# Attention with routing hidden in it: the logits' sum, the squares and the mixing moved within their units

## The chip, the cores and the metric

One core of a Trainium2 chip runs the whole program. The metric is the device time of the core in microseconds (us). The median of three runs of the kernel before is 892.65 us (891.91 to 894.43).

## What is computed

The reference is attention with a memory term, followed by two layers of experts:

```python
scores = scale * q @ k.T                      # 4 batches, 8 heads, 576 rows, depth 64; causal mask
a = softmax(scores); local = a @ v
mem_out = (phi(q) @ M_prev) / (phi(q) @ z_prev + 1e-6)   # phi(x) = max(x, 0) + exp(min(x, 0))
x = g * mem_out + (1 - g) * local             # 2304 rows of 512
# first layer: logits = (x / |x|) @ (emb / |emb|).T / tau, 8 experts; the best expert per row
# second layer: logits = x @ w_gate; both: gate * (relu(x @ w1[e]) @ w2[e])
```

## The kernel before

The attention stage works on 16 pairs of heads (four batches of four pairs). A pair has ten units: its rows are cut in four chunks of 128 and one of 64 leftover rows, and each chunk is taken for the two heads in turn, in the order 4, 0, 3, 2, 1, where chunk 4 is the leftover one. The unit numbers run on over all pairs, ten to a pair. All instructions of the stage are issued in an order written out by hand: for each step `s` the letters of one string are gone through, and each letter issues the work of one phase for the unit that has reached it.

- `s`: the scores of unit `s` on TensorE (`pss`), and the masked minimum on VectorE (`mins`, L209; it subtracts, masks and reduces in one instruction).
- `x`: the exponential of unit `s-1` on ScalarE (L244).
- `n`: the reciprocal of the row sums of a pair, two steps after its last unit.
- `a`: unit `s-3`: transposes of the exponentials on TensorE (`psat`, L261) and their copy on ScalarE (`att`, L263).
- `v`: unit `s-4`: the value product on TensorE (`psav`, L284). At the pair's third unit the leftover rows' value product (`pslo`, L281: ten float32 products, each two instructions) stands in front; its fifth and tenth product read that unit's own copy `att`, the others an earlier one.
- `c`: five steps behind: the mixing. For the leftover rows (`emit_combl`) four small VectorE steps on `pslo` and an addition; for the whole pair (`emit_comb`) a multiplication of the value product by the reciprocals on VectorE (`tmp`, L295) and the addition of the memory term on GpSimd (`xb`, L296). After a batch's last pair SyncE stores the mixed rows (L344).
- `e` and `p`: events on the other engines and on TensorE, filed under a step: loads, transposes of q and k on VectorE (L138), phi on GpSimd and ScalarE (L142, L146, L148), the memory product (`psm`, L165) and its division on VectorE (`memx`, L184), and the routing of the batch before.

Each engine takes its instructions in the order in which they were issued. The events share two PSUM slots (tag `t`) in turn: a new user waits until the last user of its slot has been read. `pslo` takes one of these slots too, in phase `v`.

The routing of the first layer for a batch is filed in `Hooks.events` for the first three batches, counted from `base`, the step in which the batch's last pair is mixed: squares of the rows on ScalarE (L1024), a square root on GpSimd (`norm1`), six VectorE steps (`norm2`), the logits as parts and their sum (`parts_pe`, `sum_pe`) with a copy (L962), five steps of `choose`, the ranks (`rank_pe`, `rank_ev`), the count (L652, L653), and seven steps of `gates`, whose first ends in a tanh on ScalarE (L626). The third batch (`last`) goes on to pick the most wanted expert (`pick_pe`, `pick`, `pick_last`), to place its rows (`place_`), to load its weights and to gather its rows. `steps(s, g, n, per)` files a generator's steps, `per` of them in each unit. The fourth batch has squares of its own, filed one unit after its third pair's mixing, at the end of `events`.

After attention come the two layers of experts, one group of 128 rows after another, bound by TensorE.

Of the kernel before, what the change touches and what calls it, by code (L numbers as in the profile page):

```python
# [20 lines left out]
def tile_attention(tc, q, k, v, M_prev, z_prev, beta, ident, x1, xp, hooks):  # L21

    nc = tc.nc
# [352 lines left out]

    W = dict(a=do_at, c=do_comb, s=do_s, x=do_exp, n=do_norm, e=do_ew, p=do_pe, v=do_av)
    for s in range(-24, U + LC + 1):
        for f in "ceaspnvx":
            W[f](s)  # L380
    ctx.close()
    pctx.close()
# [3 lines left out]
def tile_kernel(ctx, tc, q, k, v, M_prev, z_prev, beta, emb, tau, w1a, w2a, wg, w1b, w2b, out):  # L386
    nc = tc.nc
    B, H, S, D = q.shape
    E, DM, FF = w1a.shape
# [106 lines left out]
    def rtile(shape, nm, dt=F32):  # L496
        return rt.tile(shape, dt, tag=nm, name=nm)
# [60 lines left out]
    def place_(c0, n):  # L558

        sl = slice(c0, c0 + n)  # L560
        ri = rtile([P, 8], "ri", I32)[:, 0:n]
        r2 = rtile([P, 8], "r2", I32)[:, 0:n]
        rk = rtile([P, 8], "rk")[:, 0:n]
        V = nc.vector
        V.tensor_copy(ri, rkb[:, sl])
        yield
        V.tensor_scalar(out=r2, in0=ri, scalar1=7, scalar2=None, op0=ALU.arith_shift_right)
        yield
        V.tensor_scalar(out=ri, in0=ri, scalar1=127, scalar2=None, op0=ALU.bitwise_and)
        yield  # L570
        V.tensor_copy(tq[:, sl], r2)
        yield
        V.tensor_copy(rk, ri)
        yield
        V.tensor_tensor(out=ohp[:, sl], in0=iop.unsqueeze(1).to_broadcast([P, n, P]), in1=rk.unsqueeze(2).to_broadcast([P, n, P]), op=ALU.is_equal)
# [82 lines left out]
    is0, not0, isl, oth = (rtile([P, E], x) for x in ("is0", "not0", "isl", "oth"))  # L658
# [5 lines left out]
    def pick(L, cnt):  # L664

        V = nc.vector
        m0, k8 = rtile([P, 2], "m0"), rtile([P, E], "k8")
        V.tensor_reduce(out=m0[:, 0:1], in_=cnt, axis=AX.X, op=ALU.max)
        yield
        V.scalar_tensor_tensor(out=k8, in0=cnt, scalar=m0[:, 0:1], in1=ioer, op0=ALU.is_equal, op1=ALU.mult)  # L670
        V.tensor_scalar(out=nl3, in0=thr, scalar1=m0[:, 0:1], scalar2=0.0, op0=ALU.is_ge, op1=ALU.add, accum_out=nul)
        yield

        V.scalar_tensor_tensor(out=q3, in0=nl3, scalar=-99.0, in1=iot[:, 0:NE], op0=ALU.mult, op1=ALU.add)
        V.tensor_reduce(out=m0[:, 1:2], in_=k8, axis=AX.X, op=ALU.max)
        yield
        V.tensor_scalar(out=is0, in0=k8, scalar1=m0[:, 1:2], scalar2=None, op0=ALU.is_equal)
        V.tensor_scalar(out=not0, in0=k8, scalar1=m0[:, 1:2], scalar2=None, op0=ALU.not_equal)
        V.tensor_scalar(out=ini[:, L, 0:1], in0=m0[:, 1:2], scalar1=-1.0, scalar2=float(E), op0=ALU.mult, op1=ALU.add)

    def pick_last(cnt):
        V = nc.vector
        m0, k8 = rtile([P, 2], "m0"), rtile([P, E], "k8")
        V.tensor_tensor(out=k8, in0=cnt, in1=not0, op=ALU.mult)
        yield
        V.tensor_reduce(out=m0[:, 0:1], in_=k8, axis=AX.X, op=ALU.max)
        yield
        V.scalar_tensor_tensor(out=k8, in0=k8, scalar=m0[:, 0:1], in1=ioer, op0=ALU.is_equal, op1=ALU.mult)
        yield
        V.tensor_reduce(out=m0[:, 1:2], in_=k8, axis=AX.X, op=ALU.max)  # L690
        yield
        V.scalar_tensor_tensor(out=isl, in0=k8, scalar=m0[:, 1:2], in1=not0, op0=ALU.is_equal, op1=ALU.mult)
        yield
        V.tensor_tensor(out=oth, in0=not0, in1=isl, op=ALU.subtract)
# [223 lines left out]
    class Hooks:  # L918
        def events(self, pe, ew, o, ps_t, at, xb_t, xl_t):

            self.ps = {}
            self.xT = {}
            self.xb_t, self.xl_t = xb_t, xl_t
            slot = lambda nm: ps_t.tile([P, 512], F32, tag="t", name=nm)
            g = setup_gates(ps_t, xp)
            ew(1, g[0])
            ew(12, g[1])
            ew(18, g[2])
            pe(25, g[3])
            ew(26, g[4])  # L930
            for i, f in enumerate(consts()):
                ew(20 + i, f)
            for pi in range(4 * B - 1):
                b, n = divmod(pi, 4)
                sc = 10 * pi + o
                pe(sc + 6, lambda b=b, n=n: self.x_pe(b, n, slot("psxt")))
                ew(sc + 6 + 1, lambda b=b, n=n: self.x_ev(b, n, 1))
                if b % 2 == 1 and n > 0:
                    ns = range(n - 1 if n == 1 else n, n + 1)
                    d = 5 if n < KD - 1 else 4  # L940
                    pe(sc + d, lambda b=b, ns=ns: self.xl_pe(b, ns, slot("psxl")))
                    ew(sc + d + 1, lambda b=b, ns=ns: self.xl_ev(b, ns, 1))
            for b in range(B - 1):
                base = 10 * (4 * b + 3) + o
                r = Route1(*self.cols(b))
                r.rows = self.rows(b)
                for i in range(r.n):
                    ew(base + (1 + i if i < 4 else 4), lambda b=b, i=i: self.square(b, i))
                ew(base + 6, r.norm1)
                pe(base + 8, lambda b=b: self.parts_pe(b, slot("pslp")))  # L950
                ew(base + 9, lambda b=b: self.parts_ev(b))
                pe(base + 11, lambda b=b: self.sum_pe(b, slot("pslg")))

                last = b == B - 2

                def steps(s, g, n, per=1):
                    for i in range(-(-n // per)):
                        m = min(per, n - per * i)
                        ew(s + i, lambda m=m: [next(g, None) for _ in range(m)])

                lg = r.d8
                ew(base + 12, lambda b=b, lg=lg: nc.vector.tensor_copy(lg, self.lg(b)))  # L962
                steps(base + 13, r.choose(lg), 5)
                steps(base + 7, r.norm2(), 6)
                pe(base + 18, lambda r=r: r.rank_pe(slot("psr")))
                ew(base + 19, r.count)
                steps(base + 19, r.rank_ev(), 2)
                steps(base + (16 if last else 21), r.gates(), 7)
                if last:
                    steps(base + 21, place_(r.i0, r.n), 6, 2)  # L970
                    pe(base + 19, lambda: self.pick_pe(slot("pspk")))
                    cnt = oth
                    ew(base + 20, lambda: nc.vector.tensor_copy(cnt, self.ps["pk"][:, 0:E]))
                    steps(base + 21, pick(0, cnt), 4)
                    ew(base + 25, self.first_expert)
                    for c in range(8):
                        ew(base + 25 + c, lambda c=c: self.first_load(c))
                    steps(base + 25, pick_last(cnt), 6)
                    g = self.g = early(0, r.i0 + r.n, self.idx_ps)
                    steps(base + 25, g, 5)  # L980
                    pe(base + 30, lambda: self.idx_pe(slot("psid")))
                    ew(base + 31, lambda: drain(self.g))
                    ew(base + 32, lambda: gather(0, 0))
                else:
                    steps(base + 28, place_(r.i0, r.n), 6)

            b = B - 1
            pe(10 * (4 * b + 1) + o + 9, lambda: self.part_pe(slot("pslp")))
            ew(10 * (4 * b + 1) + o + 9 + 1, self.part_ev)
            for i in range(5):  # L990
                ew(10 * (4 * b + 2) + o + 1 + i, lambda i=i: self.square(b, i, slice(0, P * (KD - 1))))
# [146 lines left out]
    def rows_of(t):  # L1138

        return xgt[t % 2] if t else xg0  # L1140

    def gather(L, t):
        rows = src[L] if t >= NE else src[L][0:1 + P * (NT1 - (5, 2)[L])]
        return nc.gpsimd.indirect_dma_start(out=rows_of(t), out_offset=None, in_=rows, in_offset=bass.IndirectOffsetOnAxis(ap=idx[:, L, t:t + 1], axis=0))  # L1144

    def drain(g):
        for _ in g:
            pass

    xca = [ctile([P, 4], f"xca{i}") for i in range(2)]  # L1150
    xcb = ctile([P, 4], "xcb")
    hooks = Hooks()
    tile_attention(tc, q, k, v, M_prev, z_prev, beta, ident, x1[:, 0:DM], xp, hooks)


# [30 lines left out]
    steps = {}  # L1186
# [355 lines left out]
    b = Bufs(lambda i: Wh[0][:, 1, 512 * i:512 * i + 512] if i < 6 else None)  # L1542
# [89 lines left out]
    s, b, c = steps[1, 0], bufs, NS - 1  # L1632
# [107 lines left out]
```

## Time and profile before

| | |
|---|---|
| median of the runs | 892.65 us |
| the profiled execution | 894.2 us, its span 892.4 us |
| TensorE busy (share of the span) | 858.1 us (96%) |
| VectorE busy | 507.8 us (57%) |
| ScalarE busy | 474.4 us (53%) |
| GpSimd busy | 276.4 us (31%) |
| mean granted TensorE clock | 0.990 of full speed |

PE is TensorE (PEld its weight loads), DVE VectorE, ACT ScalarE, POOL GpSimd, SP SyncE. An idle time in brackets is that of the engine just before the instruction, with the instruction that ended it; L1024 is line 1024. Matmuls are pipelined, and the ends in their rows are modelled.

### The profile page before, as it was taken

Reading aid. Unit: us, or ns where it says so; the run is one execution under the profiler, and the core shown is the slowest. Engines: PE = TensorE matmul, PEld = TensorE weight load, DVE = VectorE, ACT = ScalarE, POOL = GpSimd, SP = SyncE. Lnnn points to the kernel's source line nnn. Section 1 sums busy time; section 2 is a strip of 40 time slices with the busy share of each in tenths; the row PEclk is TensorE's granted clock in tenths of the full one; section 3 lists DMA queues with packets and bytes.
Section 4 is the critical chain, followed back from the end, with each engine's and each line's share of the span. In section 5 each row is a group of like instructions: output and inputs, shape, how many; then the busy total and the mean of one; then the engine's idle time right before and its main releaser. Section 6 shows DMA issues by size and latency. Waiting matters only on the chain. (4 is left out here: it accounts for less than half of the span.)

```text
span 892.4 us, 20618 instructions
## 1 busy us (share of the span) xinstructions
PE 858.1 (96%) x5187; PEld 675.0 (76%) x5187; DVE 507.8 (57%) x1589; ACT 474.4 (53%) x940; POOL 276.4 (31%) x375
## 2 busy tenths in 40 slices
PE   5999999999999999999999999999989999999996
PEld 2777677777668777877888877877868888888885
DVE  5657567568575866387536676644466414463520
ACT  3657657667566635376545545432366425564531
POOL 5457636536531111221221221211132112321221
PEclk9999999999999999999999999999999999999998
DMA  8424453423215266188424317022688415384111
GB/s 131 82 44 95 79 169 94 83 45 84 55 23 204 71 225 214 49 270 274 145 79 127 106 47 228 27 51 56 220 264 276 139 48 156 128 303 131 44 38 40
DMA packets 139813, 110.30 MB, mean 124 GB/s; under 512 B 107258, under 2 KB 107258, under 8 KB 139652
## 3 DMA queue, kind: packets, MB, share of 16 engines
q1 hardware_dynamic: 129252, 85.03, 33.3%
q0 software_dynamic: 8032, 23.22, 7.9%
q8 instruction: 53, 0.87, 0.4%
q14 instruction: 108, 0.88, 0.3%
q10 hardware_dynamic: 2368, 0.30, 0.2%
HBM read 90.32 MB, written 19.25 MB: 123 GB/s over the span
## 5 line engine op out<-in xcount | busy, mean ns | idle before, releaser
L1235 PE MATMUL py<-Wh,b 128*128 (+1 forms) x688 | 240.7, 406 | 2.5 <-DVE b L1179 2.4
L1235 PE MATMUL ph<-Wh,b 128*128 (+1 forms) x672 | 227.9, 400 | 0.7 <-ACTq L1246 0.7
L901 DVE TENSOR_TENSOR Wl<-stg,Wh 128x1024 f32 (+1 forms) x120 | 145.4, 1224 | 81.7 <-ACT Wh L898 71.7
L1235 PEld LDWEIGHTS py<-Wh,b 128*128 128x128 f32 x688 | 129.3, 188 | 32.5 <-issue 4.7
L1235 PEld LDWEIGHTS ph<-Wh,b 128*128 128x128 f32 x672 | 126.8, 189 | 27.1 <-ACTq L1246 1.1
L898 ACT ACTIVATE Wh<-stg 128x1024 f32 (+1 forms) x120 | 125.6, 1058 | 25.9 <-DVEq L1246 7.5
L1235 PE MATMUL py<-Wl,b 128*128 (+1 forms) x344 | 134.8, 392 | 0.0
L1235 PE MATMUL ph<-Wl,b 128*128 (+1 forms) x336 | 131.9, 392 | 2.1 <-DVEq L1246 2.0
L1179 DVE TENSOR_TENSOR b<-pt,b 128x512 fp32r<-128x512 f32 x86 | 59.4, 691 | 104.1 <-ACT b L1178 103.2
L263 ACT ACTIVATE att<-psat 128x512 f32<-128x512 f32 (+1 forms) x144 | 66.6, 463 | 78.2 <-PE psat L261 77.4
L284 PE MATMUL psav<-vb,att 128*128 128x128 f32 (+1 forms) x640 | 97.6, 283 | 0.9 <-ACT att L263 0.8
L284 PEld LDWEIGHTS psav<-vb,att 128*128 128x128 f32 x640 | 81.7, 192 | 20.9 <-ACT att L263 9.9
L1342 POOL DMA_INDIRECT out_dram<-ysb,xca x21 | 26.9, 1282 | 192.4 <-ACTq L1246 122.9
L1178 ACT ACTIVATE b<-pt 128x512 fp32r<-128x512 f32 x86 | 51.5, 598 | 62.9 <-PE pt L1347 61.7
L244 ACT ACTIVATE a<-a,mx 128x128 f32<-128x128 f32 (+3 forms) x128 | 71.0, 555 | 9.6 <-DVE mx L209 9.6
L1235 PEld LDWEIGHTS ph<-Wl,b 128*128 128x128 f32 x336 | 63.7, 190 | 14.8 <-DVEq L1246 2.7
L1235 PEld LDWEIGHTS py<-Wl,b 128*128 128x128 f32 x344 | 64.9, 189 | 9.8
L1337 ACT ACTIVATE ysb<-py,xca 128x512 f32<-128x512 f32 x42 | 28.8, 686 | 76.1 <-PE py L1235 65.4
L1144 POOL DMA_INDIRECT xg<-x_scratch,idx x48 | 55.9, 1165 | 40.5 <-POOL xca L1331 11.2
L209 DVE CUSTOM_DVE_ANT_0 a<-pss,wmask 128x128 f32<-128x128 f32 (+3 forms) x128 | 60.6, 478 | 9.0 <-PE pss L231 6.7
L1459 POOL DMA_DIRECT2D x_scratch<-xcb x21 | 11.9, 566 | 163.4 <-DVEq L1246 61.6
L261 PE MATMUL psat<-ident,a 128*128 128x128 f32 x320 | 58.2, 280 | 0.7 <-ACT a L244 0.6
(376 smaller groups left out, 1246.5 us busy)
## 6 DMA issues: line engine op xcount, KB each, us to landing
stg<-in_moe_w_dram SPq DMA_DIRECT2D x120, 512.0 KB, 4.9
x_scratch<-ysb POOLq DMA_DIRECT2D x22, 256.0 KB, 2.8
qkn<-in_q_dram SPq DMA_DIRECT2D x64, 72.0 KB, 2.5
qkn<-in_k_dram SPq DMA_DIRECT2D x60, 72.0 KB, 2.4
vb<-in_v_dram SPq DMA_DIRECT2D x32, 128.0 KB, 2.3
x_scratch<-xb SPq DMA_DIRECT2D x16, 256.0 KB, 3.3
x_scratch<-stg SPq DMA_DIRECT2D x11, 258.0 KB, 3.8
xg<-x_scratch,idx POOLq DMA_INDIRECT x48, 4.1
```

The lines of the kernel that those rows point to most:

```text
L209: nc.vector.tensor_tensor_reduce(out=out, in0=ps, in1=mask, scale=-0.125, scalar=bound, op0=ALU.add, op1=ALU.min, accum_out=m)
L244: nc.scalar.activation(out=a[:, 0:N], in_=a[:, 0:N], func=AF.Exp, scale=-1.0, bias=mx, accum_out=rs_t[pi][:, c, j:j + 1])
L261: nc.tensor.transpose(ps[:, 128 * i:128 * i + 128], x, ident)
L263: nc.scalar.activation(out=att[:, 0:N], in_=ps[:, 0:N], func=AF.Copy)
L284: nc.tensor.matmul(av_t[pi][:, c, j:], att[:, 128 * kb:128 * kb + 128], vn[:, kb, j:, 0:D], start=(kb == 0), stop=(kb == c))
L898: return nc.scalar.activation(out=chunk(Wh, c, wv), in_=stg[:, c].unsqueeze(1), func=AF.Copy).ins
L901: return nc.vector.tensor_tensor(out=chunk(Wl, c, wv), in0=stg[:, c].unsqueeze(1), in1=chunk(Wh, c, wv).bitcast(F32), op=ALU.subtract).ins
L1144: return nc.gpsimd.indirect_dma_start(out=rows_of(t), out_offset=None, in_=rows, in_offset=bass.IndirectOffsetOnAxis(ap=idx[:, L, t:t + 1] ...
L1178: nc.scalar.activation(out=hi, in_=ps, func=AF.Copy)
L1179: nc.vector.tensor_tensor(out=lo, in0=ps, in1=hi.bitcast(F32), op=ALU.subtract)
L1235: mm = nc.tensor.matmul(ps, x[:, col:col + P], W, start=(first and q_ == qs[0]), stop=(last and q_ == qs[-1]))
L1337: nc.scalar.activation(out=ysb, in_=py, func=AF.Copy, scale=xc[:, 0:1])
```

## The change

Three things are moved; no arithmetic changes. Step numbers count from `base`.

- The order of the phases in a step is `eascpnvx` instead of `ceaspnvx`: the mixing `c` is issued behind the unit's scores and masked minimum, the events `e` come first.
- The squares stand at 1, 3, 5, 7 and 9 instead of 1, 2, 3, 4 and 4; the square root at 11 instead of 6, `norm2` from 12 instead of 7.
- The sum of the logits stands at 13 instead of 11, its copy at 14, `choose` from 15 instead of 13; in the third batch it takes two steps a unit. The ranks stand at 20 (17 in the third batch) instead of 18, `rank_ev` and the count one unit later, `gates` from 21 (18 in the third batch, two steps a unit, instead of 16). In the third batch the pick stands at 18 instead of 19, and all behind it one unit sooner.

```diff
-        for f in "ceaspnvx":
+        for f in "eascpnvx":
...
-                    ew(base + (1 + i if i < 4 else 4), lambda b=b, i=i: self.square(b, i))
-                ew(base + 6, r.norm1)
+                    ew(base + 1 + 2 * i, lambda b=b, i=i: self.square(b, i))
+                ew(base + 11, r.norm1)
...
-                pe(base + 11, lambda b=b: self.sum_pe(b, slot("pslg")))
+                pe(base + 13, lambda b=b: self.sum_pe(b, slot("pslg")))
...
+                steps(base + 12, r.norm2(), 6)
                 lg = r.d8
-                ew(base + 12, lambda b=b, lg=lg: nc.vector.tensor_copy(lg, self.lg(b)))
-                steps(base + 13, r.choose(lg), 5)
-                steps(base + 7, r.norm2(), 6)
-                pe(base + 18, lambda r=r: r.rank_pe(slot("psr")))
-                ew(base + 19, r.count)
-                steps(base + 19, r.rank_ev(), 2)
-                steps(base + (16 if last else 21), r.gates(), 7)
+                ew(base + 14, lambda b=b, lg=lg: nc.vector.tensor_copy(lg, self.lg(b)))
+                steps(base + 15, r.choose(lg), 5, 2 if last else 1)
+                k = base + (17 if last else 20)
+                pe(k, lambda r=r: r.rank_pe(slot("psr")))
+                steps(k + 1, r.rank_ev(), 2, 2 if last else 1)
+                ew(k + 1, r.count)
+                steps(base + (18 if last else 21), r.gates(), 7, 2 if last else 1)
                 if last:
-                    steps(base + 21, place_(r.i0, r.n), 6, 2)
-                    pe(base + 19, lambda: self.pick_pe(slot("pspk")))
+                    pe(base + 18, lambda: self.pick_pe(slot("pspk")))
...
-                    steps(base + 21, pick(0, cnt), 4)
+                    steps(base + 20, pick(0, oth), 4)
+                    steps(base + 20, place_(r.i0, r.n), 6, 2)
...
```

## Rows read from the trace of the kernel before

**Rows 1.** Stages view, the attention stage: stretch, its length, busy time (instructions), clock, DMA

```profile
24.00:288.00 264.00, 258.84 (x2034) 192.42 (x2032) 174.23 (x702) 172.04 (x483) 137.14 (x169) 0.99 0.38 88
```

**Rows 2.** Waits of TensorE, 24 to 290 us: us in total, times, longest

```profile
PE pslo L281 <- PE pss L231: 1.5, 2, 1.0
PE pslo L281 <- issue: 1.4, 1, 1.4
PE psav L284 <- ACT att L263: 0.8, 1, 0.8
PE psat L261 <- ACT a L244: 0.6, 2, 0.4
PE pss L231 <- DVE mx L209: 0.3, 1, 0.3
PE psm L165 <- DVE memx L184: 0.3, 1, 0.3
```

**Rows 3.** Stages view, 235 to 245 us; the clock is third from the end

```profile
235.00:240.00 5.00, 3.59 (x29) 2.88 (x28) 4.51 (x15) 2.63 (x7) 5.00 (x5) 0.89 0.05 11
240.00:245.00 5.00, 5.00 (x39) 4.38 (x39) 2.51 (x10) 2.12 (x6) 2.24 (x4) 0.77 0.01 3
```

**Rows 4.** Timeline of all engines, 82 to 86 us: first batch's last mixing and first square

```profile
82.18 0.69 DVE L295 TENSOR_TENSOR tmp<-psav,rs 128x512 f32<-128x512 f32 x1 [1.27 <-PE psav L284]
82.51 1.13 PE L231 MATMUL pss<-kT,qT 64*128 64x512 f32 x4
...
82.96 1.28 POOL L296 TENSOR_TENSOR xb<-tmp,memx 128x512 f32<-128x512 f32 x1 [5.11 <-DVE rn L176]
...
83.57 0.33 PE L261 MATMUL psat<-ident,a 128*128 128x128 f32 x1
...
84.20 1.67 POOL L142 TENSOR_SCALAR ph<-qT 128x576 f32<-128x576 f32 x1
84.20 0.69 DVE L209 CUSTOM_DVE_ANT_0 a<-pss,wmask 128x512 f32<-128x512 f32 x1
84.27 0.63 ACT L1024 ACTIVATE mv<-xb 128x512 bf16<-128x512 f32 x1 [0.61 <-POOL xb L296]
...
84.81 0.77 DVE L138 STREAM_TRANSPOSE kT<-qkn 128x576 f32<-128x576 f32 x1
84.90 0.36 ACT L263 ACTIVATE att<-psat 128x256 f32<-128x256 f32 x1
...
85.79 0.62 PE L281 MATMUL pslo<-vb,att 128*64 128x65 f32 x7
```

**Rows 5.** Timeline of TensorE, first and third batch's pslo: start, us, instruction, idle before

```profile
104.65 1.35 PE L281 MATMUL pslo<-vb,att 128*64 128x65 f32 x20 [0.96 <-PE pss L231]
107.40 0.49 PE L231 MATMUL pss<-kT,qT 64*128 64x256 f32 x2
...
239.11 2.40 PE L281 MATMUL pslo<-vb,att 128*64 128x65 f32 x20 [1.41 <-issue]
...
243.33 0.49 PE L231 MATMUL pss<-kT,qT 64*128 64x256 f32 x2
```

**Rows 6.** Timeline, 187 to 189 us: second batch's first step of the gates

```profile
187.60 0.16 DVE L625 TENSOR_TENSOR d<-d,sc 128x40 f32<-128x40 f32 x1
...
187.94 0.37 ACT L263 ACTIVATE att<-psat 128x256 f32<-128x256 f32 x1
188.18 0.62 PE L281 MATMUL pslo<-vb,att 128*64 128x65 f32 x7
```

**Rows 7.** Timeline, 250 to 259 us: third batch's ranks and count, then a placing step

```profile
250.23 0.78 DVE L138 STREAM_TRANSPOSE qT<-qkn 128x576 f32<-128x576 f32 x1
...
250.75 0.19 PE L617 MATMUL psr<-oh,tri 128*128 128x32 bf16 x1
...
251.32 0.20 DVE L652 TENSOR_REDUCE ca<-oh 128x8 f32<-128x32 bf16 x1
...
251.63 0.17 DVE L653 TENSOR_TENSOR acc<-acc,ca 128x8 bf16<-128x8 bf16 x1
251.71 0.18 DVE L645 TENSOR_TENSOR t<-oh,psr 128x32 f32<-128x32 bf16 x1
...
258.77 0.98 DVE L569 TENSOR_SCALAR ri<-ri 128x4 int32<-128x4 int32 x1
```

More of the change, by code (lines that the diff above doesn't have):

```diff
@@ L968, in events @@
-                steps(base + (16 if last else 21), r.gates(), 7)
-                if last:
-                    steps(base + 21, place_(r.i0, r.n), 6, 2)
-                    pe(base + 19, lambda: self.pick_pe(slot("pspk")))
-                    cnt = oth
-                    ew(base + 20, lambda: nc.vector.tensor_copy(cnt, self.ps["pk"][:, 0:E]))
-                    steps(base + 21, pick(0, cnt), 4)
-                    ew(base + 25, self.first_expert)
+                ew(base + 14, lambda b=b, lg=lg: nc.vector.tensor_copy(lg, self.lg(b)))
@@ new lines, in events @@
+                steps(base + 15, r.choose(lg), 5, 2 if last else 1)
[4 more added lines that the diff above has]
+                steps(base + (18 if last else 21), r.gates(), 7, 2 if last else 1)
+                if last:
+                    pe(base + 18, lambda: self.pick_pe(slot("pspk")))
+                    ew(base + 19, lambda: nc.vector.tensor_copy(oth, self.ps["pk"][:, 0:E]))
+                    steps(base + 20, pick(0, oth), 4)
+                    steps(base + 20, place_(r.i0, r.n), 6, 2)
+                    ew(base + 24, self.first_expert)
@@ L976, in events @@
                     for c in range(8):
-                        ew(base + 25 + c, lambda c=c: self.first_load(c))
-                    steps(base + 25, pick_last(cnt), 6)
+                        ew(base + 24 + c, lambda c=c: self.first_load(c))
+                    steps(base + 24, pick_last(oth), 6)
                     g = self.g = early(0, r.i0 + r.n, self.idx_ps)
-                    steps(base + 25, g, 5)
-                    pe(base + 30, lambda: self.idx_pe(slot("psid")))
-                    ew(base + 31, lambda: drain(self.g))
@@ L983, in events @@
-                    ew(base + 32, lambda: gather(0, 0))
+                    steps(base + 24, g, 5)
+                    pe(base + 29, lambda: self.idx_pe(slot("psid")))
+                    ew(base + 30, lambda: drain(self.g))
+                    ew(base + 31, lambda: gather(0, 0))
                 else:
```

## The prediction

> **What bounds the kernel now.** I first read the page's shares: TensorE is busy 96% of the span, no other engine over 57%. Then the attention stage alone [rows 1]: 258.84 of 264 us, and all that the diff moves is issued there, so only TensorE's gaps in that stage count. The view of waits names them [rows 2]: three waits of the leftover rows' value product (pslo), 2.9 us together, one of a value product for a copied attention tile (0.8), and three small ones of 0.3 to 0.4 in the third batch's routing. One pslo wait (0.5) stands at a place that the diff leaves alone. The chain of waits I left aside: it ends in the last stage, at work that merely runs earlier or later with the end of attention. Last the clock [rows 3]: 1.00, then 0.89 and 0.77 in the two stretches behind the longest gap, a piece of some 3.4 us at the lower level (0.11 and 0.23 of 5 us, doubled).
>
> What a gap is worth: TensorE works in order, so a gap that goes moves the end by itself, unless another comes behind it. An idle time in these rows counts from the modelled end of the matmul before. The next could have started sooner, as in [rows 4], where the product at 82.51 ends by its row at 83.64 and its successor runs on time at 83.57. By starts the gaps are 0.1 to 0.4 longer; for the six gaps below I add 1.0 us in all (estimate).
>
> **Logits' sum two units later.** pslo, sum and the memory product share two PSUM slots in turn. With the sum in front, pslo takes the slot of the second memory product, which VectorE has yet to read; behind it, pslo takes the first one's, read two units before. Away go 0.96 us in the first batch and 1.41 in the third [rows 5]; the second shows none, since five tiles' logits stand there as cover. What is late next is the sum: its slot is read in the unit before it, so I cost it at nothing (if that read ran late, at most the old 0.96). The sum's matmuls are the same ones. Behind the 1.41 gap came the slow stretch: from pslo to the next scores 4.22 us, against 2.75 in the first batch, whose gap of 0.96 left the clock full [rows 5]. I let the drop go: 1.47 us more. Bounds: 0 if another drop replaces it, 1.47.
> The Trainium skill (TensorE: Matmul & The Clock Gate, HAM oscillation) takes half of the throttled time as the loss. By that rule the 3.4 us would give 1.7 instead of the rows' 1.47, and the sum would be 0.2 us better.
>
> **Squares in every other unit.** In the second batch they stood four units in a row and two in one unit, and the 0.8 us wait for ScalarE's copy came there [rows 2]. Apart, this goes: 0.77. Three like it, under the view's threshold, I leave to the range (0.1 to 0.3 each). The square root, normalization and choice come up to six units later; nothing on TensorE waits for them before the ranks.
>
> **Mixing behind the minimum.** This is the costly part. In the unit that is `base`, VectorE mixed at 82.18, GpSimd added till 84.24, and the first square, at the head of ScalarE's next unit, waited for that add [rows 4]. Behind it in ScalarE's queue stands the attention copy at 84.90, done at 85.26. The leftover product reads it with its ninth matmul of twenty (20 take 1.35 [rows 5], so 0.5 after the first): needed at 86.3, a spare 1.0 us.
> Now the mixing stands behind the minimum. The scores end at 83.64, the minimum starts at 83.70 and hands on after 0.61 (84.20 to 84.81): mixing at 84.31, 2.13 later. Add 0.78 later and 1.28 long, to 86.37; the copy starts 0.66 after that (84.24 to 84.90), takes 0.36, ends 87.39. TensorE waits from 86.3: 1.1 us. GpSimd's own `min` (1.67), which now precedes the add, fits in the 5.11 us idle. There are three such places, one a batch; the same steps from the mixings at 149.44 and 216.12 give 1.3 and 1.1: 3.5 in sum. The fourth batch's squares, which the diff leaves as they are, also begin one unit after a mixing (273.02); that stretch ran at the lower clock, so between 0 and 1.3, taken 0.7. Bounds for all four: 0 to 5. Elsewhere a later mixing is read six units on: nothing. Minima start up to 1 us sooner, which no wait of TensorE asks for outside the third batch. SyncE's four stores of the mixed rows start 2.1 us later and the value loads behind them too, ten units ahead of use: nothing.
>
> **Gates, ranks, count.** The gates' tanh heads ScalarE's unit, again ahead of the copy that pslo reads. In the second batch VectorE gave it at 187.60, the copy ended at 188.31 and was needed at 188.7: 0.35 spare [rows 6]. In front of it now come the mixing (0.69; the minimum, bound by its scores, can't move up) and the rank's product and the count's two steps (251.32 to 251.71 and 0.1: 0.5) [rows 7]. 1.2 less 0.35 is 0.85. In the first batch the minimum can move up 0.7, and the same sum leaves 0.4. So 1.3; bounds 0 to 2.
> Third batch: the pick's matmul comes in the unit of the count. TensorE is there some 0.15 us after 250.75; VectorE transposes from 250.23 for 0.7, then rank and count end near 251.65 [rows 7]: 0.8 us of wait, bounds 0.4 to 1. In exchange the three waits of 0.3, 0.3 and 0.4 [rows 2] are redrawn: the one-hot rows and small steps (some 1.5 us) now precede the minimum for which the scores wait, some 0.9 us of other steps come earlier. I let the three go (1.0) and put one wait of 1.0 in their place, bounds 0.5 to 1.9. First weight loads and the gather start a unit sooner on SyncE's and GpSimd's queues; nothing reads them before attention ends, so I cost them at nothing.
> VectorE's small steps have a second price too: 0.98 us for four elements a partition at 258.77, where eight at 251.63 take 0.17 [rows 7]. GpSimd was multiplying at that time. The normalization now runs in the units in which GpSimd works without pause.
> The Trainium skill (SBUF — State Buffer, Who interferes with whom) has VectorE and GpSimd share a port pair under an exclusive lock. [...]
> I put this at nothing, since VectorE's minima there have about 1.5 us before their copies are asked for (estimate), and keep 3 us as a bound.
>
> **Sum.** Gained: gaps 0.96 + 1.41 + 0.77 + 1.0 = 4.14, by starts 1.0 more, clock 1.47: 6.6. Lost: 3.5 + 0.7 + 1.3 + 0.8 + 1.0 = 7.3. Net 0.7 slower. The profiled execution took 894.2 us (span 892.4 and 1.8 around it), so 894.9 there. It is 1.55 above the median of the runs, about the price of one stretch at the lower clock; on the median of 892.65 the forecast is **893.3 us**, no change that can be told: 0.3%, about 2.7 us, is what a measurement of this kernel can tell from none.
>
> **Rivals.**
> 1. *The squares' wait is hidden, faster.* If TensorE has other work there, or the add comes sooner, 3.5 + 0.7 are not paid: 893.3 - 4.2 = 889.1. For it: ScalarE waited 0.61 us for this add before and TensorE none. Against: only 1.0 us was spare, and the shift is twice that. Chance 0.15.
> 2. *The new gaps drop the clock, slower.* Five new gaps of about 1 us stand where work was dense. A gap of 1.41 was followed by the lower clock, one of 0.96 was not; the new ones lie between, and two more drops would cost 2.9: 896.2. It decides at the first pslo behind a square. Chance 0.12.
> 3. *VectorE locked out beside GpSimd, slower.* Six normalization steps in each of three batches; if one in three takes 0.8 us more (0.98 less 0.17) in front of a minimum and half reaches TensorE: 6 x 0.8 / 2 = 2.4, to 895.7. Chance 0.08. The rule named above would bring this about.
> 4. *The change doesn't do what it says.* pslo still waits in the first and third batch, for the copy or another slot, and the drop stays: 0.96 + 1.41 + 1.47 come back, 897.1. Chance 0.08.
> The forecast has 0.57; by its own bounds it lies from 891 to 895.5.
>
> **How the numbers follow.** The range runs from 889.2, which all but reaches rival 1, to 896.8, over rivals 2 and 3. Faster: 0.14 of rival 1 and 0.02 of the forecast, 0.16. Slower: rivals 2 and 4, half of 3, and 0.01 of the forecast, 0.25. Within 0.3%: the rest, 0.59.
>
> **What would show it.** Right: no idle time before pslo at the unit of the old 104.65 and 239.11; the square's row with an idle time of about 2.7 us released by GpSimd's add, and behind it pslo split with a gap of about 1 us, three times; the pick's matmul waiting for VectorE's acc; clock 1.00 around 235 to 245. Wrong: pslo unbroken behind the squares (rival 1), or more stretches at the lower clock than before (rival 2).

## The result, and the profile after

| | before | new kernel |
|---|---|---|
| median of the runs | 892.43 us (891.91 to 894.43, 4 runs) | 901.2 us (899.8 to 901.37, 4 runs) |
| ratio to before, 95% interval | | 1.0091 [1.0072, 1.0109] |
| profiled execution, its span | 894.2, 892.4 us | 901.37, 899.6 us |
| TensorE busy | 858.1 us | 859.0 us |
| first attention score to the next stage's first matmul | 279.4 us | 286.5 us |

The forecast was 893.3 us, its range ended at 896.8. TensorE does the same work; 7.0 of the 7.2 us by which the spans differ were lost in the attention stage. In its stages view (stretch, length, busy time and instructions of TensorE, its weight loads, VectorE, ScalarE, GpSimd; clock, DMA share, GB/s) the stretch is 7 us longer than in [rows 1], TensorE busy for as long as there:

```profile
24.00:295.00 271.00, 259.29 (x2030) 192.06 (x2029) 176.01 (x699) 170.69 (x482) 139.29 (x169) 0.99 0.37 86
```

The new kernel's waits of TensorE, the same view as [rows 2] (us in total, times, longest):

```profile
PE pslo L281 <- ACT att L263: 4.6, 5, 1.2
PE psat L261 <- ACT a L244: 1.8, 6, 0.8
PE pslp L1050 <- DVE memx L184: 1.2, 1, 1.2
PE pss L231 <- DVE mx L209: 1.2, 1, 1.2
PE pslo L281 <- issue: 1.1, 1, 1.1
PE pspk L662 <- DVE acc L653: 1.0, 1, 1.0
PE psm L165 <- POOL mz L157: 0.6, 1, 0.6
```

The old list added up to 4.9 us, this one to 11.5. None of the old large waits is in it: pslo's waits for its slot in the first and third batch and the 0.8 for a copied tile are gone. But the leftover product now waits five times for ScalarE's copy.

In the timeline of TensorE the first and the third batch's pslo run without idle time and at full speed (1.38 us in place of the 2.40 in [rows 5]), with the sum behind them:

```profile
104.85 1.38 PE L281 MATMUL pslo<-vb,att 128*64 128x65 f32 x20
...
106.92 0.96 PE L1068 MATMUL pslg<-sel,xT 128*128 128x8 f32 x8
...
241.55 1.38 PE L281 MATMUL pslo<-vb,att 128*64 128x65 f32 x20
...
243.62 0.96 PE L1068 MATMUL pslg<-sel,xT 128*128 128x8 f32 x8
```

The all-engine timeline of the place of [rows 4], the unit behind the first batch's last pair:

```profile
83.49 1.13 PE L231 MATMUL pss<-kT,qT 64*128 64x512 f32 x4
...
84.65 0.69 DVE L209 CUSTOM_DVE_ANT_0 a<-pss,wmask 128x512 f32<-128x512 f32 x1 [0.69 <-PE pss L231]
...
85.27 0.69 DVE L295 TENSOR_TENSOR tmp<-psav,rs 128x512 f32<-128x512 f32 x1
...
86.04 1.27 POOL L296 TENSOR_TENSOR xb<-tmp,memx 128x512 f32<-128x512 f32 x1 [2.62 <-DVE tmp L295]
...
86.55 0.68 PE L281 MATMUL pslo<-vb,att 128*64 128x65 f32 x8
...
87.34 0.63 ACT L1024 ACTIVATE mv<-xb 128x512 bf16<-128x512 f32 x1 [2.71 <-POOL rkb L448]
...
87.97 0.36 ACT L263 ACTIVATE att<-psat 128x256 f32<-128x256 f32 x1
...
88.39 0.91 PE L281 MATMUL pslo<-vb,att 128*64 128x65 f32 x12 [1.16 <-ACT att L263]
```

Read it from the bottom: the last twelve matmuls wait for the copy, the copy stands behind the square, the square behind GpSimd's add (it ends at 87.31), the add behind the mixing, the mixing behind the minimum, the minimum behind the scores. (The square's row names a memset of rkb, which stands directly behind the add. In E3 below the square runs 1.65 us ahead of that memset, so it is the add that counts.) The mixing starts 1.78 us behind the start of the unit's scores, where in [rows 4] it stood 0.33 ahead of it. Of these 2.1 us about 0.6 are the minimum itself, and the other 1.5 its wait for the scores. The same gap stands at 156.00 (1.17) and 225.08 (1.16).

Where it went, pair by pair: the time from one pair's first score matmul to the next pair's (us; the last to the next stage's first matmul), worked out from the traces of five kernels, E2, E5 and E10 being experiments below. E10's trace is of its slowest run (890.64 us at a mean clock of 0.990), while six of its eight runs lie between 885.8 and 887.3 us at 0.993 or more, so its column holds more of the lower clock than its median does. Pairs with less than 0.1 us of difference between before and new are left out.

| pair | what stands there | before | new | E2 | E5 | E10 |
|---|---|---|---|---|---|---|
| 2 | unit 26, slot of the second memory product | 16.57 | 17.17 | 17.16 | 16.57 | 16.56 |
| 4 | first square, batch 1 | 16.22 | 17.31 | 17.31 | 16.05 | 16.04 |
| 5 | pslo and sum, batch 1 | 18.35 | 17.41 | 17.41 | 17.40 | 17.40 |
| 6, 7 | ranks and tanh, batch 1 | 32.69 | 32.89 | 32.89 | 32.02 | 32.02 |
| 8 | first square, batch 2 | 16.96 | 17.38 | 17.37 | 15.59 | 15.58 |
| 9 | fifth square, sum, batch 2 | 18.25 | 19.13 | 19.14 | 19.14 | 18.30 |
| 10 | ranks and tanh, batch 2 | 15.79 | 16.95 | 16.95 | 16.08 | 16.07 |
| 12 | first square, batch 3 | 16.20 | 17.31 | 17.31 | 16.05 | 16.05 |
| 13 | pslo and sum, batch 3 | 20.36 | 17.41 | 17.40 | 17.41 | 17.41 |
| 14 | pick, placing, batch 3 | 18.11 | 19.89 | 21.54 | 19.30 | 18.97 |
| 15 | index product, batch 4's squares | 22.83 | 26.55 | 22.81 | 23.55 | 24.47 |

Pairs 5 and 13 give back 3.9 us, as forecast; all others lose 10.9. In pairs 14 and 15 the clock moves as well: 3.4 us at half in pair 15 before, 6.8 in pair 15 of the new kernel and of E10, 3.4 in pair 14 of E2 and in pair 15 of E5. In the new kernel's stages view it is these two rows (clock third from the end; 0.27 and 0.41 of 5 us, doubled, are 6.8 us):

```profile
275.00:280.00 5.00, 4.59 (x30) 4.29 (x32) 0.78 (x4) 0.02 (x1) 0.00 (x0) 0.73 0.93 348
280.00:285.00 5.00, 5.00 (x19) 2.62 (x20) 2.85 (x9) 1.35 (x4) 1.51 (x2) 0.59 0.03 11
```

So the attention stage holds as much of the lower clock as before: 3.4 us in pair 13 and 3.4 in pair 15 there, 6.8 in pair 15 here.

Three of the places had no term in the sum. The fifth square, moved to `base + 9`, reads the second batch's leftover rows xl (one buffer); GpSimd's add into xl waits for it, behind the add stands a multiply for the memory product:

```profile
166.85 0.62 ACT L1024 ACTIVATE mv<-xl 128x512 bf16<-128x512 f32 x1
...
167.63 0.45 POOL L296 TENSOR_TENSOR xl<-tmp,memx 64x128 f32<-64x128 f32 x1 [7.96 <-ACT mv L1024]
...
168.05 0.39 POOL L157 TENSOR_TENSOR mz<-mz,gt 128x128 f32<-128x128 f32 x1
...
168.49 0.86 PE L165 MATMUL psm<-mz,ph 128*128 128x130 f32 x4 [0.57 <-POOL mz L157]
```

The index product, a unit sooner, shares its unit with the memory product and the fourth batch's partial logits (L1050): three users of two PSUM slots, so the third waits for VectorE to read the first's (memx, 274.64 for 0.62). TensorE's rows:

```profile
273.08 0.75 PE L165 MATMUL psm<-mz,ph 128*128 128x130 f32 x4
273.76 0.48 PE L714 MATMUL psid<-mvh,ohp 128*128 128x6 bf16 x13
275.41 2.68 PE L1050 MATMUL pslp<-enT,xT 128*128 128x8 f32 x20 [1.16 <-DVE memx L184]
```

And unit 26, where the wait of 0.52 us that I had left out of account, the diff being elsewhere, became 1.12: VectorE now mixes ahead of the reading of that slot.

```profile
54.87 0.56 DVE L184 TENSOR_TENSOR memx<-psm,rn 128x384 f32<-128x384 f32 x1
...
55.53 1.35 PE L281 MATMUL pslo<-vb,att 128*64 128x65 f32 x20 [1.12 <-issue]
```

### The profile page after: what moved, and what is told of

Read it like the earlier page. It is cut to its first block, busy times and chain, and to the rows that moved or that the text cites. A ratio compares the mean times of both kernels' runs of the same rounds, so it can differ in the third digit from the quotient of the medians.

```text
span 899.6 us, 20635 instructions
## 1 busy us (share of the span) xinstructions
PE 859.0 (95%) x5187; PEld 675.2 (75%) x5187; DVE 509.8 (57%) x1589; ACT 473.2 (53%) x940; POOL 277.4 (31%) x375
```

## The experiments

Theory A: the later mixing is the cost, and the rest of the change is a gain. Rivals: the routing's new units are the cost (B); single steps of it are (slot, fifth square, pick). The kernel before was timed again on the chips of the experiments (medians 893.9 to 894.1 us), so ratios are what to compare. Diffs are against the new kernel unless it is said otherwise.

**E1, the order alone, in the kernel before.**

```diff
-        for f in "ceaspnvx":
+        for f in "eascpnvx":
```

> The kernel before with nothing but the order of the phases of the change (events first, mixing behind the minimum). Theory A (the later mixing is the main cost: the first square of a batch waits for it on ScalarE, and pslo for ScalarE, 1.2 to 1.4 us in each of three batches, and VectorE reads the memory products later): 897 to 899 us, with pslo split by a gap of about 1.1 us behind the first square of each batch. Theory B (the main cost is the third batch's routing, packed two steps a unit and with one more user of the two PSUM slots in unit 153): within 1 us of the kernel before, 892 to 893.5.

Measured: 904.32 us, ratio 1.0127 [1.0101, 1.0153]. A, and more than its 897 to 899 us: by the medians the order alone costs more than the whole change, though the intervals touch. Its waits of TensorE:

```profile
PE pslo L281 <- ACT att L263: 4.9, 5, 1.2
PE pslo L281 <- issue: 4.1, 3, 1.5
...
```

The waits for the slot that the later sum removes (0.96 and 1.41 before) are 1.47 each here. The lower clock comes four times in attention, against twice before: behind both of these waits (107.5 and 250.9 us), and at 179.2 and 285.0.

**E2, the index product, its drain and the gather a unit later (as before).**

```diff
-                    pe(base + 29, lambda: self.idx_pe(slot("psid")))
-                    ew(base + 30, lambda: drain(self.g))
-                    ew(base + 31, lambda: gather(0, 0))
+                    pe(base + 30, lambda: self.idx_pe(slot("psid")))
+                    ew(base + 31, lambda: drain(self.g))
+                    ew(base + 32, lambda: gather(0, 0))
```

> The changed kernel with the index product, its reading and the gather back where they were (one unit later), nothing else. Theory B: in the changed kernel unit 153 has three users for two PSUM slots, and the fourth batch's partial logits wait 1.16 us for VectorE there, and the clock then falls for 6.8 us. So the gap before L1050 goes and the lower clock with it or half of it: 897.5 to 899 against 901.2. Theory A: the gap goes, the clock falls all the same (it did before, in 3.4 us): 899.5 to 900.

Measured: 898.06 us, ratio 1.0060 [1.0036, 1.0084], against 1.0091: about 3 us, though the intervals overlap and within its theory B's 897.5 to 899 (B is the slot here). By the traces it is 2.1 us in pairs 1 to 15, and 1.5 of it is the lower clock. The wait of 1.16 us in front of L1050 is gone and pair 15 has no stretch at the lower clock; one of 3.4 us stands in pair 14 instead. With this wait gone the fourth batch's square shows its own gap, 0.72 us in pslo at 282.53.

**E3, E2 with the old order of the unit.**

```diff
-        for f in "eascpnvx":
+        for f in "ceaspnvx":
```

> As e2, and with the old order of the phases too (mixing first). Against e2: Theory A: 5 us faster or more, 893 to 894.5, no gap within pslo behind the squares, no wait before the pslo of unit 26 beyond the 0.5 us of before. Theory B: within 1.5 us of e2.

Measured: 889.53 us, ratio 0.9964 [0.9945, 0.9983]: faster than the kernel before, and 8.5 us below E2. That is theory A, though its 893 to 894.5 us was some 4 us too high. No pslo is split behind a square or a tanh beyond 0.2 us, unit 26 waits 0.52 us as before. What is left, by its waits of TensorE:

```profile
PE pss L231 <- DVE mx L209: 1.5, 2, 1.1
PE pspk L662 <- DVE acc L653: 0.7, 1, 0.7
PE psid L714 <- DVE memx L184: 0.6, 1, 0.6
...
```

**E4, the fifth square at its old unit.**

```diff
-                    ew(base + 1 + 2 * i, lambda b=b, i=i: self.square(b, i))
+                    ew(base + (1 + 2 * i if i < 4 else 4), lambda b=b, i=i: self.square(b, i))
```

> The changed kernel with the square of the leftover rows back at base + 4. Theory: the leftover rows of all batches share one buffer, so that GpSimd's addition for the next batch waits for this square, and GpSimd's scaling of the memory term behind it came late: a gap of 0.57 us before psm in the second batch. It goes: 0.6 us faster than the change, 900.6. Rival: the gap has another cause (the normalization) and stays: 901.2.

Measured: 900.27 us, ratio 1.0082 [1.0056, 1.0108]. Against the new kernel's 1.0091 this can't be told by time; by the trace the wait of psm is gone and pair 9 takes 18.30 us in place of 19.13, while pair 8, where the square now stands, takes 0.27 more.

**E5, E2 with the mixing between the attention copies and the minimum.**

```diff
-        for f in "eascpnvx":
+        for f in "eacspnvx":
```

> E2 (the new kernel, index product, its copy and its gather a unit later: 898.1 us, ratio 1.006) with the mixing put between the attention's copy and the unit's masked minimum, so that it still stands behind the routing's steps but no longer behind the minimum; E3 has it ahead of all three (889.5 us, ratio .9964). Theory A1: it is the masked minimum alone, some 1.2 us of VectorE ahead of the mixing and of everything read behind it, that costs the 8.5 us: the time comes to 889 to 891 us and the half-clock stretches and the gaps within the leftover product go as in E3. Rival A2: the routing's steps ahead of the mixing cost as much, since a square or a small step then also delays it: 893 to 896 us. Rival A3: any place behind the routing's steps costs it all: 897 to 899 us.

Measured: 889.12 us, ratio 0.9954 [0.9937, 0.9971]: A1. That the mixing stands behind the routing's steps costs nothing that can be told from E3; that it stands behind the minimum costs all. One stretch at the lower clock is left (3.4 us in pair 15), against A1's words. Its waits of TensorE have no copy behind a square any more:

```profile
PE pspk L662 <- DVE acc L653: 1.0, 1, 1.0
PE pss L231 <- DVE mx L209: 0.9, 1, 0.9
PE psat L261 <- ACT a L244: 0.8, 4, 0.2
...
```

The minimum itself takes 0.69 us. The larger part of the price is its wait for the scores (1.5 us at the place shown above): everything queued behind it on VectorE waits too.

**E6, the first four squares one unit later.**

```diff
-                    ew(base + 1 + 2 * i, lambda b=b, i=i: self.square(b, i))
+                    ew(base + (2 + 2 * i if i < 4 else 9), lambda b=b, i=i: self.square(b, i))
```

> The new kernel with the first four squares of a batch one unit later each (units 2, 4, 6, 8 behind the base in place of 1, 3, 5, 7; the fifth stays at 9). Theory A: the three gaps of 1.16 us within the leftover product come from the first square alone, which now stands in the unit of the mixing and ahead of the attention's copy; with it out of that unit they and the .2 us gaps behind them go, 3 x (1.16 + .2) = 4.1 us, and the time comes to 896.5 to 898 us against 901.2. Rival: the copy of the next unit waits for the square as long, the gap only moves, 900 to 902 us. Also under theory A: the tanh split, the unit-26 wait of 1.12 us and the third batch's tail stay as they are.

Measured: 896.05 us, ratio 1.0040 [1.0016, 1.0065]: theory A, just below its 896.5. Pairs 4, 8 and 12 take 15.77, 15.84 and 15.77 us: 1.54 less each, 4.6 in all. In the timeline pslo is whole, and the square, which now comes behind the copy that pslo reads, has kept ScalarE idle for 0.58 us where it was 2.71:

```profile
84.28 1.28 POOL L296 TENSOR_TENSOR xb<-tmp,memx 128x512 f32<-128x512 f32 x1 [2.62 <-DVE tmp L295]
...
84.79 1.38 PE L281 MATMUL pslo<-vb,att 128*64 128x65 f32 x20
...
85.60 0.63 ACT L1024 ACTIVATE mv<-xb 128x512 bf16<-128x512 f32 x1 [0.58 <-POOL rkb L448]
```

**E7, E2 with the pick and all behind it a unit later too (as before).**

```diff
-                    pe(base + 18, lambda: self.pick_pe(slot("pspk")))
-                    ew(base + 19, lambda: nc.vector.tensor_copy(oth, self.ps["pk"][:, 0:E]))
-                    steps(base + 20, pick(0, oth), 4)
-                    steps(base + 20, place_(r.i0, r.n), 6, 2)
+                    pe(base + 19, lambda: self.pick_pe(slot("pspk")))
+                    ew(base + 20, lambda: nc.vector.tensor_copy(oth, self.ps["pk"][:, 0:E]))
+                    steps(base + 21, pick(0, oth), 4)
+                    steps(base + 21, place_(r.i0, r.n), 6, 2)
...
```

> The new kernel with the pick of the third batch, what stands behind it and the index product each one unit later, as in the kernel before (order of the unit unchanged). Includes E2's edit, which alone gave 898.1 us. Theory A: the pick's wait of .97 us at 253.8 goes or falls to .3, the third batch's two late waits (.76 and 1.15 us) fall by at least half, and the time comes to 896 to 897.3 us. Rival: these waits come from the mixing behind the minimum and from the choice two units apart, not from the pick's place: no change against E2, 897.7 to 898.5 us.

Measured: 895.93 us, ratio 1.0024 [1.0011, 1.0037]. Theory A, at its lower end. The pick's wait is gone: the 0.26 us that E9's text below puts down to it stands in front of the value product behind the pick, which waits for an attention copy. The scores' wait fell from 1.15 to 0.56, that of the transposes only from 0.76 to 0.69. Pair 14 takes 18.93 us (21.54 in E2, with 3.4 us at the lower clock that are gone too).

**E8, E7 with the old order and the fifth square at its old unit** (the edits of E3 and E4).

> E7's steps with the kernel before's order of the unit (mixing ahead), the first four squares in every other unit as in the new kernel, the fifth back at its old place four units behind the base. So from E3 (889.5 us, ratio .9964) the waits that are left and have a cause go: .57 us of the memory product's transposes behind the fifth square and .73 us of the pick. Theory A: 888.0 to 888.8 us, ratio .994 to .9955, faster than both kernels. Rival: the third batch's waits behind the pick (1.09 us) grow as all of it is later, and the fifth square gives a gap of its own: 889.5 to 891 us.

Measured: 889.21 us, ratio 0.9953 [0.9935, 0.9971]; no lower than E5. The waits aimed at are gone (the pick has none), but the profiled execution shows the lower clock at 174.0 (3.4 us) and 269.5 (6.8 us). By its time it lies between the theory's 888.8 and the rival's 889.5, by its ratio within the theory's .994 to .9955: the run does not decide between them.

**E9, E7 with the order of E5, and E10, E9 with the fifth square a unit sooner.**

```diff
-                    ew(base + 1 + 2 * i, lambda b=b, i=i: self.square(b, i))
+                    ew(base + (1 + 2 * i if i < 4 else 8), lambda b=b, i=i: self.square(b, i))
```

> E5 (mixing ahead of the minimum but behind the routing's steps, index product a unit later: 889.1 us, ratio .9954) with the third batch's pick and what stands behind it a unit later, as in E7; the fifth square stays at nine units behind the base. Theory: E7 showed that this takes the pick's wait (.97 to .26 us) and one of 1.15 us down to .56; here .97 and .93 stand, so about 1 us goes: 887.5 to 888.7 us, ratio .993 to .995. Rival: as in E8 (889.2), where the same step brought stretches at the lower clock in its place: 889 to 890 us.

> E9 with the fifth square one unit sooner (eight units behind the base in place of nine), so that GpSimd's add into the leftover rows' tile is let go earlier and the .57 us wait of the memory product in the second batch goes or halves: .3 to .8 us below E9. Rival: two units in a row with a square at the head of ScalarE's queue give a split leftover product of their own: same as E9 or up to .5 us above.

Measured: E9 888.15 us, ratio 0.9943 [0.9921, 0.9964], as expected; E10 886.65 us, ratio 0.9914 [0.9897, 0.9930], **faster than both kernels**. The step between them is larger than expected, but the intervals overlap; the trace shows pair 9 at 18.30 us instead of 19.14. E10's waits of TensorE:

```profile
PE psat L261 <- ACT a L244: 1.2, 5, 0.4
PE pslo L281 <- PE pss L231: 0.5, 1, 0.5
PE pss L231 <- DVE mx L209: 0.3, 1, 0.3
PE psav L284 <- ACT att L263: 0.3, 1, 0.3
```

**E11, E3 with squares and normalization at their old units**, so that only the sum and what follows it is moved.

```diff
-                    ew(base + 1 + 2 * i, lambda b=b, i=i: self.square(b, i))
-                ew(base + 11, r.norm1)
+                    ew(base + (1 + i if i < 4 else 4), lambda b=b, i=i: self.square(b, i))
+                ew(base + 6, r.norm1)
...
-                steps(base + 12, r.norm2(), 6)
+                steps(base + 7, r.norm2(), 6)
```

> E3 (old order of the unit, ratio .9964) with the squares and the normalization back at their old units, so against the kernel before only the logits' sum, its copy, the choice, the ranks and the third batch's pick are re-timed. Theory: the gain of E3 is the sum's: the waits of .96 and 1.41 us in front of the leftover product and the half-clock stretch behind the second go, the .77 us wait behind the four squares in a row stays: 889.8 to 891 us, ratio .9965 to .998. Rival: it is the squares in every other unit that gain: 892 to 894 us, no difference to the kernel before.

Measured: 893.77 us, ratio 0.9997 [0.9985, 1.0009]: my theory missed. By the trace the sum did what it should (pairs 5 and 13: 17.80 and 17.80 us, 3.1 less than before), and the third batch's pick and placing gave 1.6 of it back (pair 14: 19.71). What E3 has beyond it came from the squares apart: pairs 4, 8 and 12 go from 16.20, 16.96 and 16.18 to 15.73, 15.59 and 15.75, which is 2.3 us.

**E12, E2 with the leftover rows' mixing alone put ahead of the minimum.**

```diff
-        if (c, j) == (CH[1], 0):
-            emit_combl(pi)
...
-        for f in "eascpnvx":
+        for f in "ealscpnvx":
```

(`l` issues `emit_combl`.)

> E2 (order as in the new kernel, index product a unit later: 898.1 us, ratio 1.006) with the leftover rows' mixing put back ahead of the minimum, the mixing of the pair's four tiles still behind it. Theory P: the four tiles' mixing (.69 us on VectorE, 1.27 on GpSimd, then the square and the stores) is the costly one; the leftover rows' three small steps cost nothing: 896.5 to 898.5 us, gaps of 1.16 us behind the squares as in E2. Rival Q: the leftover product's PSUM slot, which its mixing sets free, is what the others wait for: 890 to 893 us and the gaps behind the tanh and at unit 26 go.

Measured: 897.77 us, ratio 1.0045 [1.0029, 1.0061], the gaps where E2 has them (86.95, 154.56, 223.65: 1.16 to 1.17 us): theory P, it is the mixing of the four tiles. (The leftover rows' mixing is three steps on VectorE, as E12's text says, not four.)

## Why the prediction was wrong

**The gains were right only in part.** Pair 5 gave 0.94 (0.96 forecast), pair 13 gave 2.95 (1.41 and the clock's 1.47: 2.88); of the 1.0 us that I added "by starts" nothing shows in these two. The squares apart gave 2.3 us instead of 0.77 (E11 against E3). And the clock's 1.47, gained in pair 13, was paid back in pair 15, where the lower clock stood for 6.8 us instead of 3.4: the bound of 0, "if another drop replaces it", is what came. The Trainium skill (TensorE: Matmul & The Clock Gate, HAM oscillation) would have put the clock at 1.7 us in place of 1.47; pair 13 less its gap, 2.95 - 1.41 = 1.54, lies between and nearer the row's number.

**The failed step is the price of the mixing behind the minimum.** The mechanism was right and its first place nearly exact: 1.1, 1.3 and 1.1 us of gap forecast, 1.16, 1.17 and 1.16 measured. But the term stood for the gap alone, and "Elsewhere a later mixing is read six units on: nothing" was wrong:
- behind each gap TensorE waits 0.2 us more, in the transposes for ScalarE's late exponential; E6 shows 1.54 us a square, 4.6 in place of 3.5, since the gains by squares apart are kept there;
- unit 26, 0.6 us: it isn't the mixing's reader that is late, but VectorE's next reading of a PSUM slot. I had traced who reads the mixing's output and not who stands behind it in VectorE's queue;
- the tanh, forecast at 1.3 us: two gaps of 0.57 and 0.58 with 0.20 behind each; E2 against E5 makes it 0.87 a batch, 1.7.

The fourth batch's square, taken at 0.7, is hidden in the new kernel by the wait in front of L1050, and is 0.72 us in E2.

E5 prices the whole step: 0.0106 x 894 = 9.5 us by the ratios, 8.3 by the traces, where the sum had 3.5 + 0.7 and part of the tanh's 1.3.

**"First weight loads and the gather start a unit sooner ... I cost them at nothing"** failed next. I looked at who reads the gather and not at the PSUM slot that the index product takes on its way: 1.16 us of wait. E2 is about 3 us faster, but 1.5 of the 2.1 us that its trace shows are the lower clock, and that this belongs to the wait is not shown: E6 has the wait and a stretch of 3.4 us behind L1050, E8 and E10 have no wait and 6.8.

**"Squares in every other unit": the fifth square** had no price, because I took its reader and not the one buffer that it holds: 0.57 us of wait, 0.8 of pair 9 by E4 and E10.

**The third batch.** The pick's wait was forecast at 0.8 us and is 0.97. The "one wait of 1.0" behind it is two, 0.76 and 1.15, at the upper bound of 1.9 that I gave. In the timeline VectorE's placing steps stand in front of the minimum, two of them stretched:

```profile
262.46 2.90 POOL L148 TENSOR_TENSOR ph<-ph 128x576 f32<-128x576 f32 x2
262.51 1.12 DVE L573 CAST rk<-ri 128x4 f32<-128x4 int32 x1
...
264.28 0.55 DVE L209 CUSTOM_DVE_ANT_0 a<-pss,wmask 128x384 f32<-128x384 f32 x1
264.76 0.08 DVE L209 DVE_READ_ACCUMULATOR2_ANT mx<- 128x1 f32 x1
264.76 0.64 DVE L677 TENSOR_SCALAR is<-k,m 128x8 f32<-128x8 f32 x1
264.88 0.61 ACT L244 ACTIVATE a<-a,mx 128x384 f32<-128x384 f32 x1 [1.98 <-DVE mx L209]
264.90 0.70 PE L231 MATMUL pss<-kT,qT 64*128 64x256 f32 x2 [1.15 <-DVE mx L209]
```

A cast of four elements takes 1.12 us beside GpSimd's multiplication (a cast of the same size 0.16 at 260.81). This is rival 3's sign, and not in the third batch only: of the eighteen normalization steps five take 0.35 to 1.00 us, the others 0.15 to 0.21. The longest, of four elements, starts at 109.02, and four of the five, as well as the cast, end 0.02 us behind a GpSimd multiplication or addition (the cast at 263.63, the first of the two multiplications at 263.61). But no wait of TensorE stands behind the normalization steps, so the rival did not decide the result; its share of the third batch's waits was not measured by itself. The Trainium skill (SBUF — State Buffer, Who interferes with whom) has a port pair shared by VectorE and GpSimd, a lock held for a whole instruction, and names the VectorE instructions that need it: those in a two-port mode and those with two inputs in SBUF. The common ends agree with such a lock, but the two-input step at 177.00 beside another GpSimd instruction (L115) takes only 0.15 us, and no run took GpSimd's work away.

**The other rivals.** Rival 1 fell: pslo was split. Rival 2 (new gaps lower the clock) fell at its own place: gaps of 1.16 us in pslo, three times, and the clock stayed full there; the lower clock stood no longer in attention than before. Rival 4 fell: the old gaps are gone.

**How the sums close, and what they leave open.** From the new kernel to E10 each step undoes one part. The table takes pairs 1 to 15 from the traces (pair 0 differs by up to 1.8 us from run to run) and subtracts 1.54 us for each 3.4 us at the lower clock; that is an estimate, by pair 13.

| kernel | pairs 1 to 15, us | at the lower clock | less the clock (estimate) |
|---|---|---|---|
| before | 258.7 | 6.8 | 255.6 |
| new | 265.7 | 6.8 | 262.6 |
| E2: index product later | 263.6 | 3.4 | 262.0 |
| E5: mixing ahead of the minimum | 255.3 | 3.4 | 253.8 |
| E9: pick later | 252.8 | 0 | 252.8 |
| E10: fifth square sooner | 255.1 | 6.8 | 252.0 |

So the steps to E10 take back 10.6 us of losses, 8.3 of them the order's, where 7.3 were forecast, 5.5 for the order (squares and tanh). What is gained without the clock, E10 against the kernel before, is 3.6 (pair 14 still loses 0.9 there), where 5.1 were forecast. And the clock gave nothing, where 1.47 were forecast. These three shortfalls, 3.3, 1.5 and 1.5, are the 6.3 us between the forecast's 0.7 and the 7.0 of the traces. The medians differ by up to 1.8 us more (8.8), which lies outside of these pairs or in other runs than the profiled ones and stays open; so does why the lower clock stood longer in pair 15. E10's median, 0.0086 x 894 = 7.7 us below the kernel before, holds some of the clock as well.

## What to carry to other kernels

When work is moved behind an instruction that waits for another engine, the price is that wait more than the instruction's length (here 1.5 and 0.6 us); charge it to everything that the mover's queue holds behind it, and to whatever reads PSUM slots and buffers there, not only to the readers of the moved result. A step that "nothing reads for a long time" still takes a slot and a buffer when it is issued: follow these too. When a bundle of moves comes out slower, undo its parts one by one before giving it up; here the place of one letter in the order, with the index product, hid a gain of 0.5% (E5).

## What was not expected of the hardware

The lower clock came without an idle time in front. In E10's stages view TensorE is busy throughout 264.5 to 274 us, and yet the clock is full (2.4 GHz) in the first row and half (1.2) in the two that follow:

```profile
264.50:267.10 2.60, 2.60 (x23) 2.30 (x21) 1.89 (x12) 0.65 (x3) 0.00 (x0) 1.00 0.97 384
267.10:270.50 3.40, 3.40 (x15) 2.72 (x16) 0.89 (x2) 0.69 (x2) 0.83 (x1) 0.51 1.05 393
270.50:274.00 3.50, 3.50 (x26) 2.15 (x22) 1.54 (x6) 2.11 (x8) 1.41 (x2) 0.51 0.61 230
```

When it fell, TensorE was in the midst of the twenty matmuls of eight columns of L1050 (265.21, 2.71 us). In the new kernel too the clock falls during these, at 277.31. In nine of the fourteen kernels traced, the one before among them, it fell during them or shortly behind; in E2, E3, E7, E9 and E12, with the same matmuls, it did not: so they go with the drop but do not settle it. The stretch at 179.2 in E1 has sixteen matmuls of eight columns and a gap of only 0.58 us in front. Behind the gaps of 1.16 us within pslo it stayed full, behind the wait of 1.41 before and the two of 1.47 in E1 it fell each time.
